# A transformer block on one Trainium2 core: a new order of tasks, q and k in three chunks, one transpose for two token streams, and load tasks tied to compute tasks

## The chip, the core and the metric

The kernel runs on one core of a Trainium2 chip. The core has five engines that run their own instruction queues and wait for each other by semaphores: PE (TensorE: a weight load, then a matmul), DVE (VectorE), ACT (ScalarE), POOL (GpSimd) and SP (SyncE, which here only issues DMAs). The metric is the device time of one execution in microseconds (us). Before the change it is 292.95 us, the median of three runs (291.63 to 293.17).

## The reference, cut to what matters

```python
S, D, H, Dh, W, dil, Fh = 2048, 448, 16, 28, 8, 2, 896
# A: sliding local attention, 8 keys at a distance of 2
q, k, v = layernorm(x) @ wqkv                    # 3 x 448 columns
logits = einsum('bhsd,bhswd->bhsw', q, k[pos - 2 * w]) * Dh ** -0.5   # masked where pos - 2w < 0
o = einsum('bhsw,bhswd->bhsd', softmax(logits), v[pos - 2 * w])
h = x + o @ wo
# B: gMLP; the tokens are mixed by a full 2048 x 2048 matrix
z = gelu(layernorm(h) @ w_in)                    # 2 x 896 columns
g = einsum('ts,bsf->btf', w_sp, layernorm(z[..., Fh:])) + b_sp[None, :, None]
out = h + (z[..., :Fh] * g) @ w_out
```

## The kernel before, in words

The 2048 tokens are two streams of 1024 (s = 0, 1), and most steps handle a **unit** u of 128 tokens of both streams at once (8 units). The steps, in the names of the program's tasks:

- `bn1`, `rs1`, `nrm1`, `tT1`, `ev1` for a unit: layernorm statistics on DVE (L612, L613), the reciprocal root on POOL (L602, L603), the normalisation into the ring `tring` on DVE (L626), transposes on PE (L636: fourteen of 64 columns, seven for each stream), and the copy into `xh` (L597 on ACT or L599 on DVE). `xh` holds stream 0 in partitions 0 to 63 and stream 1 in 64 to 127, so that a matmul over 64 rows for either stream can stand beside that of the other. 16 tokens ahead of stream 1 take the same way by themselves (`xhalo`, `thalo`, L657 to L674).
- `rpk`, `rpq`: q and k weights are copied from the staged `wqkv` into padded columns (L597, L599, and POOL's L599). `mmk`, `mmq` (L728): q and k for four groups g of heads, in chunks of 128, 256, 256, 256 and 128 tokens (`CB`), evicted by L597 or L599.
- For each of nine attention tiles i of 114 tokens: `mmv` (L768) and its eviction, `mml` (L802, 64 small matmuls: the logits), `exp` (L815, ACT), `mask` (L823, DVE), `mmr` (L832: the row sums), `mmo` (L846, 64 small matmuls), `ln` and `rex` (L856, L862, ACT: one over the sum), `ot` (L870, DVE).
- For each unit: `mmy` (L908: the product with `wo`), `h` (L916: the residual), layernorm again (`bn2`, `rs2`, `nrm2`, `tT2`, `ev2`, by the same lines), `mmz2` (L928), gelu `ge` (L938), and the layernorm of z2 (`bn3` L944, `ag3` L950, `rs3`, `nrm3` L958).
- `mmz1` (L972) and gelu `gz1` (L982); then `g` (L1009: 448 matmuls of 512 columns), `ua`, `um` (L1019, L1027), the product with `w_out` (L1038), the last addition (L1046) and the stores (L1050).

PSUM has eight banks; most steps take two at a time, so four such pairs are in play. A pair is free again when its eviction has run.

**What sets the order.** A planner (`Planner.run`) plays the tasks through with assumed durations and picks by priority; each task's instructions are then written into the queue of its engine in the order picked. A task's `deps` count in the planner alone. The semaphore waits that the chip sees are made apart from that, by `Sched.issue`, from the resources (`Res`) that an instruction reads and writes. Some resources are coarse: `reg3_old` stands for all of region `reg3` (wo, E, L and V of the attention). The loads of `b_sp` (`bb`, L990) and of `w_out` (L988) and `gz1` of f = 4 to 6 (L982) all write it, so they come one after the other. `r_wo` does the same for the four loads of `wo` (L877): each waits for the one before, and the first for a memset of the whole tile on POOL (`c_wo0`, L584).

SP issues, in this order: x, the q/k/v weights, `wo` (four DMAs), `w_in` (four, L534), sixteen transposing loads of the first half of `w_sp` (L889), `bb`, `w_out`, sixteen of the second half, the stores. ACT issues three loads at the start.

Of the kernel before, what the change touches and what calls it, by code (L numbers as in the profile page):

```python
# [1 line left out]

# [4 lines left out]
D = 448  # L7
DH = 28
FH = 896
# [3 lines left out]
NU = 8  # L13
ST = 1024
HALO = 14
# [16 lines left out]
WPEN = 40.0  # L32
# [95 lines left out]
class LazyRes:  # L128
# [6 lines left out]
    def __iter__(self):  # L135
        return iter([self.lst[self.hold[0]]])
# [28 lines left out]
class Planner:  # L165
# [4 lines left out]
    def __init__(self, pools, epochs, table_task):  # L170
        self.tasks = []
        self.pools = {k: [(0.0, s) for s in v] for k, v in pools.items()}
        self.epochs = epochs
        self.table_task = table_task

    def add(self, *a, **k):
        t = Task(*a, **k)
        self.tasks.append(t)
        return t

    def pick(self, p, n):
# [4 lines left out]
        whole = sorted((b for b in range(0, 8, 2) if b in free and b + 1 in free), key=lambda b: max(free[b], free[b + 1]))  # L186
# [19 lines left out]
    def run(self, bw=200.0, setup=1.9, t0=0.7):  # L206
# [29 lines left out]
        while ndone < len(tasks):  # L236
# [22 lines left out]
            while progress:  # L259
                progress = False  # L260
                for e in self.ENGS:
# [5 lines left out]
                    def key(t):  # L267
                        if e != "pe":
                            return t.prio
                        return t.prio + (1.5 if t.mode != pe_mode else 0.0) + WPEN * (self.pe_time(t, cr) - t.dur)  # L270
# [69 lines left out]
def bass_sequential_preLN__sliding_local_dilated__mixer_gmlp__prompt_kernel(  # L340
# [18 lines left out]
    with contextlib.ExitStack() as top:  # L359
# [3 lines left out]
        NTR = 6  # L363
        NE = 2
        NV = 3
        NL = 2
# [4 lines left out]
        tring = sb("tring", [128, NTR, D], BF16)  # L371
# [15 lines left out]
        thalo = sb("thalo", [16, D], BF16)  # L387
# [48 lines left out]
        r_tr = [Res("tr%d" % i) for i in range(NTR)]  # L436
        r_xh = [Res("xh%d" % u) for u in range(NU)]
        r_xpad0 = Res("xpad0")
        r_xpad1 = Res("xpad1")
# [4 lines left out]
        r_q = [[Res("q%d_%d" % (c, g)) for g in range(4)] for c in range(5)]  # L444
        r_k = [[Res("k%d_%d" % (c, g)) for g in range(4)] for c in range(5)]
# [38 lines left out]
        pl = Planner({"ps": range(8), "tr": range(NTR), "E": range(NE), "V": range(NV), "L": range(NL),  # L484
# [3 lines left out]
        TU = 11.0  # L488
# [74 lines left out]
        c_xpad = cst("c_xpad", [(lambda e: e.memset(xh[0:64, :, 0:HALO], 0.0), [], [r_xpad0]),  # L563
                                (lambda e: e.memset(xh[:, :, HALO + ST:XW], 0.0), [], [r_xend])], 0.4, prio=-97)
# [19 lines left out]
        c_wo0 = cst("c_wo0", [(lambda e: e.memset(wo_p[:, :, :], 0.0), [], [r_wo])], 1.65, prio=14)  # L584
# [21 lines left out]
        def ln_unit(u, which, src_deps, prio, ev_deps):  # L606
# [13 lines left out]
            tn, hold = [], []  # L620
            for n, b in enumerate(bl):
                h = []
                hold.append(h)

                def em_n(b=b, h=h):
                    iss("dve", lambda e: e.tensor_scalar(tring[:, h[0], :], x_tm[:, b, :], mv[:, b, 0:1], rs[:, b:b + 1],  # L626
                                                         ALU.subtract, ALU.mult),
                        reads=[r_x[b], rl[b]], writes=[r_tr[h[0]]])
                tn.append(add("nrm%d_%d" % (which, b), "dve", 0.31, em_n, deps=[tr], prio=prio + 0.5, acq=[("tr", 1, h)]))
            bk = []  # L630

            def em_t():
                o = bk[0] * 1024
                for c in range(NC7):
                    for s in range(2):
                        iss("pe", lambda e, c=c, s=s: e.transpose(psb[64 * s:64 * s + 64, o + 128 * c:o + 128 * c + 128],  # L636
                                                                 tring[:, hold[s][0], 64 * c:64 * c + 64], ident[:, :]),
                            reads=[r_tr[hold[s][0]], r_ident], writes=[r_bank[bk[0]]])
            tt = add("tT%d_%d" % (which, u), "pe", 0.40, em_t, deps=tn + [c_ident], prio=prio + 1.0, acq=[("ps", 1, bk)],
                     rel=[("tr", hold[0]), ("tr", hold[1])], mode="C", nmm=14)  # L640
# [10 lines left out]
        for u in range(NU):  # L651
            t_xh.append(ln_unit(u, 1, [t_x[u], t_x[u + 8]], 2.0 + 6.0 * u, ()))
            if u == 0:
                hb = []

                def em():
                    iss("dve", lambda e: e.bn_stats(sth[:, :], xhalo[:, :]), reads=[r_xhalo], writes=[r_lnh])  # L657
                    iss("dve", lambda e: e.bn_aggr(mvh[:, :], sth[:, :]), reads=[r_lnh], writes=[r_lnh])
                th = add("bnh", "dve", 0.76, em, deps=[t_xhalo], prio=9.0)
                th = add("rsh", "pool", 1.05, lambda: rstd(rsh[:, :], mvh[:, 1:2], nhalf[0:16, 0:1], [r_lnh]), deps=[th], prio=9.0)  # L660
                th = cst("nrmh", [(lambda e: e.tensor_scalar(thalo[:, :], xhalo[:, :], mvh[:, 0:1], rsh[:, 0:1], ALU.subtract, ALU.mult),
                                   [r_xhalo, r_lnh], [r_thalo])], 0.35, eng="dve", deps=[th], prio=9.5)

                def em_t():
                    o = hb[0] * 1024
                    for c in range(NC7):
                        iss("pe", lambda e, c=c: e.transpose(psb[64:128, o + 16 * c:o + 16 * c + 16],
                                                            thalo[:, 64 * c:64 * c + 64], ident[0:16, 0:16]),
                            reads=[r_thalo, r_ident], writes=[r_bank[hb[0]]])
                th = add("tTh", "pe", 0.4, em_t, deps=[th, c_ident], prio=10.0, acq=[("ps", 1, hb)], mode="C", nmm=7)  # L670

                def em_e():
                    o = hb[0] * 1024
                    iss("dve", lambda e: e.tensor_copy(xh[64:128, :, 0:HALO],  # L674
                                                       psb[64:128, o:o + 112].rearrange("p (c t) -> p c t", c=NC7)[:, :, 2:16]),
                        reads=[r_bank[hb[0]]], writes=[r_xpad1])
                t_xpad1 = add("evh", "dve", 0.17, em_e, deps=[th], prio=10.2, rel=[("ps", hb)])
# [23 lines left out]
        CB = [0, 128, 384, 640, 896]  # L701
        t_q = [[None] * 4 for _ in range(5)]
# [392 lines left out]
```

## Time and profile before

| | before |
|---|---|
| time, median of 3 runs | 292.95 us |
| the profiled execution | 293.18 us, span 291.4 us |
| PE busy | 263.4 us (90%) |
| DVE, ACT, POOL busy | 149.1, 91.4, 32.9 us |
| mean granted clock of PE | 0.940 |
| chain that ended last, by engine | PE 83%, DMA 6%, DVE 5%, issue 3%, ACT 2% |

The span runs from the first to the last instruction. A line such as `L728` is a line of the kernel before. In the chain of work, each piece has its start, its length and what it is; "issue" is time in which an engine waited for nothing that the profile shows. In the timeline, a bracket behind a row gives the idle time ahead of it and what ended it. In the windows, each row gives a stretch, its length, and the busy time of each engine with its number of instructions, then the granted clock of PE, the share of the DMA engines and GB/s.

### The profile page before, as it was taken

Reading aid. Unit: us, or ns where it says so; the run is one execution under the profiler, and the core shown is the slowest. Engines: PE = TensorE matmul, PEld = TensorE weight load, DVE = VectorE, ACT = ScalarE, POOL = GpSimd, SP = SyncE. Lnnn points to the kernel's source line nnn. Section 1 sums busy time; section 2 is a strip of 40 time slices with the busy share of each in tenths; the row PEclk is TensorE's granted clock in tenths of the full one; section 3 lists DMA queues with packets and bytes.
Section 4 is the critical chain, followed back from the end, with each engine's and each line's share of the span. In section 5 each row is a group of like instructions: output and inputs, shape, how many; then the busy total and the mean of one; then the engine's idle time right before and its main releaser. Section 6 shows DMA issues by size and latency. Waiting matters only on the chain.

```text
span 291.4 us, 7309 instructions
## 1 busy us (share of the span) xinstructions
PE 263.4 (90%) x3323; PEld 145.0 (50%) x3335; DVE 149.1 (51%) x284; ACT 91.4 (31%) x98; POOL 32.9 (11%) x78
## 2 busy tenths in 40 slices
PE   7289767998997999999938999999999999999996
PEld 2087645656765684545413444444444444444442
DVE  2886641577686865899524504333333333333333
ACT  0436833558447279763404660000000000000000
POOL 7631400012011020123110100000000000000000
PEclk9759975999999995999986999999999999999999
DMA  6946999993000000000073343333100010001001
GB/s 215 258 142 142 207 201 149 161 139 66 6 2 4 2 4 2 0 3 2 12 205 75 72 96 86 72 74 72 63 0 2 0 63 2 0 0 63 2 0 64
DMA packets 43735, 19.90 MB, mean 68 GB/s; under 512 B 34536, under 2 KB 43576, under 8 KB 43704
## 3 DMA queue, kind: packets, MB, share of 16 engines
q1 hardware_dynamic: 42632, 18.11, 30.3%
q10 hardware_dynamic: 1072, 1.32, 1.6%
q8 instruction: 26, 0.43, 0.6%
q14 instruction: 5, 0.04, 0.1%
HBM read 9.20 MB, written 1.84 MB: 38 GB/s over the span
## 4 chain that ended last, share of the span: by engine, by line
PE 83%; DMA 6%; DVE 5%; issue 3%; ACT 2%; SPq 0%; ACTq 0%
PE psum L1009 33%; PE psum L728 10%; PE psum L928 8%; PE psum L1038 7%; PE psum L972 7%; PE psum L908 4%; PE psum L768 4%; PE psum L846 3%; DMA xhalo<-in_A_x_dram 3%; PE psum L636 2%; PE psum L802 2%; DMA reg<-in_B_w_out_dram 2%; DVE reg L599 2%; DMA reg<-in_B_b_sp_dram 1%; PE psum L832 1%
## 5 line engine op out<-in xcount | busy, mean ns | idle before, releaser
L1019 DVE TENSOR_TENSOR ub<-psum,reg 128x512 bf16<-128x512 f32 x28 | 19.4, 692 | 71.5 <-PE psum L1009 71.5
L1009 PE MATMUL psum<-reg,z2p 128*128 128x512 bf16 x218 | 48.5, 379 | 0.3
L1009 PE MATMUL psum<-wspT_lo,z2p 128*128 128x512 bf16 x218 | 48.2, 379 | 0.5 <-issue 0.3
L1009 PEld LDWEIGHTS psum<-reg,z2p 128*128 128x128 bf16 x224 | 21.9, 98 | 26.4
L1009 PEld LDWEIGHTS psum<-wspT_lo,z2p 128*128 128x128 bf16 x224 | 21.6, 98 | 26.6 <-issue 0.8
L728 PE MATMUL psum<-xh,reg 64*128 64x256 bf16 (+2 forms) x560 | 31.8, 273 | 0.6 <-DVE xh L674 0.3
L928 PE MATMUL psum<-w_in,xh 64*128 64x448 bf16 x224 | 25.1, 384 | 5.3 <-ACT reg L982 5.3
L728 PEld LDWEIGHTS psum<-xh,reg 64*128 64x128 bf16 x560 | 25.0, 105 | 5.0 <-issue 0.8
L597 ACT ACTIVATE reg<-psum 128x1024 bf16<-128x1024 f32 (+2 forms) x19 | 17.0, 895 | 27.3 <-PE psum L728 17.0
L944 DVE BATCH_NORM_STATS2 st<-z2p 128x6 f32<-128x448 bf16 x32 | 17.9, 611 | 8.9 <-ACT z2p L938 8.9
L972 PE MATMUL psum<-xh,w_in 64*128 64x512 bf16 x196 | 21.9, 376 | 0.0
L1038 PE MATMUL psum<-reg 128*128 128x448 bf16 x112 | 21.8, 352 | 0.0
L602 POOL TENSOR_SCALAR rs<-mv 128x2 f32<-128x2 f32 x24 | 7.1, 297 | 126.7 <-DVE mv L613 87.9
L612 DVE BATCH_NORM_STATS2 st<-x_tm 128x6 f32<-128x448 bf16 x32 | 19.4, 605 | 2.0 <-DMA x_tm<-in_A_x_dram 1.9
L928 PEld LDWEIGHTS psum<-w_in,xh 64*128 64x128 bf16 x224 | 11.3, 102 | 18.1 <-ACT reg L982 6.0
L982 ACT ACTIVATE reg<-psum 128x1024 bf16<-128x1024 f32 x14 | 14.3, 1024 | 17.9 <-PE psum L972 10.9
L815 ACT ACTIVATE reg<-psum 128x928 bf16<-128x928 f32 x18 | 17.0, 943 | 7.8 <-PE psum L768 3.8
L603 POOL TENSOR_TENSOR rs<-rs,nhalf 128x2 f32<-128x2 f32 x24 | 17.1, 713 | 2.0
L938 ACT ACTIVATE z2p<-psum 128x896 bf16<-128x896 f32 x16 | 14.7, 917 | 7.1 <-PE psum L928 7.1
L1038 PEld LDWEIGHTS psum<-reg 128*128 128x128 bf16 x112 | 11.0, 98 | 10.4
L636 PE MATMUL psum<-ident,tring 128*64 128x128 bf16 x224 | 10.5, 239 | 6.0 <-issue 3.1
L626 DVE TENSOR_SCALAR tring<-x_tm,mv,rs 128x448 bf16<-128x448 bf16 x32 | 12.6, 432 | 6.1 <-POOL rs L603 6.0
(62 smaller groups left out, 242.9 us busy)
## 6 DMA issues: line engine op xcount, KB each, us to landing
w_in<-in_B_w_in_dram SPq DMA_DIRECT2D x4, 784.0 KB, 12.3
out_dram<-tring SPq DMA_DIRECT2D x16, 112.0 KB, 1.7
x_tm<-in_A_x_dram SPq DMA_DIRECT2D x15, 112.0 KB, 8.0
z2p<-in_A_wqkv_dram ACTq DMA_DIRECT2D x1, 784.0 KB, 7.9
z2p<-in_A_wqkv_dram SPq DMA_DIRECT2D x1, 784.0 KB, 9.4
reg<-in_B_w_out_dram SPq DMA_DIRECT2D x1, 784.0 KB, 4.8
reg<-in_B_b_sp_dram SPq DMA_DIRECT2D x1, 512.0 KB, 3.7
reg<-in_A_wqkv_dram ACTq DMA_DIRECT2D x1, 392.0 KB, 10.2
```

What stands on the lines that cost most here:

```text
L597: iss("act", lambda e: e.activation(dst, src, AF.Copy), reads=rd, writes=wr)
L603: iss("pool", lambda e: e.tensor_tensor(dst, dst, nh, ALU.pow), reads=rr + [r_nhalf], writes=rr)
L612: iss("dve", lambda e: e.bn_stats(st[:, b, :], x_tm[:, b, :]), reads=[r_x[b]], writes=[rl[b]])
L636: iss("pe", lambda e, c=c, s=s: e.transpose(psb[64 * s:64 * s + 64, o + 128 * c:o + 128 * c + 128], tring[:, hold[s][0], 64 * c:64 * c + 6 ...
L728: iss("pe", lambda e, c=c, s=s, gi=gi, lhs=lhs: e.matmul(psum[:, bk[s] * 512 + cw * gi:bk[s] * 512 + cw * gi + cw], lhs, xh[64 * s:64 * s ...
L815: iss("act", lambda e: e.activation(E[:, es[0], 2 * n:2 * n + 2, :], pair_view(lb, 2 * n, 8 * JW), AF.Exp, scale=SCALE), reads=[r_bank[lb[ ...
L928: iss("pe", lambda e, c=c, s=s: e.matmul(psum[:, zb[s] * 512:zb[s] * 512 + D], xh[64 * s:64 * s + 64, c, HALO + 128 * u:HALO + 128 * u + 128],
L944: iss("dve", lambda e, b=b: e.bn_stats(st3[:, b, k, :], z2p[:, b, D * k:D * k + D]), reads=[r_z2[b][k]], writes=[r_st3[b][k]])
L972: iss("pe", lambda e, c=c, s=s: e.matmul(psum[:, bk[s] * 512:bk[s] * 512 + 512], w_in[64 * s:64 * s + 64, c, 128 * f:128 * f + 128], xh[64 ...
L1009: iss("pe", lambda e, b=b: e.matmul(psum[:, gb[0] * 512:gb[0] * 512 + 512], z2p[:, b, 128 * f:128 * f + 128], src[:, b, 512 * (tc % 2):512 ...
L1019: iss("dve", lambda e: e.tensor_tensor(ub[:, us_[0], :], psum[:, gb[0] * 512:gb[0] * 512 + 512], bb[:, 512 * tc:512 * tc + 512], ALU.add), ...
L1038: iss("pe", lambda e, f=f: e.matmul(psum[:, wb[0] * 512:wb[0] * 512 + D], z1p[f][:, 128 * m:128 * m + 128], w_out[:, f, :], start=(f == 0) ...
```

## The change

- The priorities of nearly all tasks are moved by a table of offsets (`OFF`) and by a seeded random number; the tiles' due times lie closer (`TU` 11.0 to 7.616). The planner's costs of a change of mode and of issue-bound work on PE are higher (`MPEN`, `WPEN`).
- q and k are made in three chunks (128, 384 or 398, 512 tokens) instead of five.
- A unit's two streams are normalised into one row of `tring`, 64 columns of one beside 64 of the other, and seven transposes of 128 columns take the place of fourteen of 64.
- The four banks of the logits are taken and freed as two pairs.
- `mmo` is planned behind `ln`; the memset `c_wo0` behind the second unit's `ev1`.
- Each load of `w_in`, `w_sp`, `bb` and `w_out` gets one compute task as a dependency in the planner.

```diff
-WPEN = 40.0
+WPEN = 189.727
+MPEN = 4.564
+OFF = {"q": -19.2, "v": -12.23, "evv": -0.37, "l": -69.19, "exp": 78.83, "mask": -16.37, "r": -86.03,
+       "o": -57.86, "ln": -12.7, "ot": 3.28, "y": 6.26, "h": 35.75, "ln2": -14.24, "z2": 28.29, "ge": -10.62,
+       "n3": 22.43, "x0": 11.12, "xd": 1.15, "evq": 37.45}
+SEED, SIGMA = 806416, 0.5
+O_AFTER_LN = True
+TU = 7.616
...
     def add(self, *a, **k):
         t = Task(*a, **k)
+        if SIGMA and t.eng != "sp":
+            t.prio += self.rng.gauss(0.0, SIGMA)
...
-        NTR = 6
+        NTR = 4
-        tring = sb("tring", [128, NTR, D], BF16)
+        tring = sb("tring", [128, NTR, 2 * D], BF16)
...
-        c_wo0 = cst("c_wo0", [(lambda e: e.memset(wo_p[:, :, :], 0.0), [], [r_wo])], 1.65, prio=14)
+        c_wo0 = cst("c_wo0", [(lambda e: e.memset(wo_p[:, :, :], 0.0), [], [r_wo])], 1.65, prio=50, deps=[t_xh[1]])
...
-                    for s in range(2):
-                        iss("pe", lambda e, c=c, s=s: e.transpose(psb[64 * s:64 * s + 64, o + 128 * c:o + 128 * c + 128],
-                                                                 tring[:, hold[s][0], 64 * c:64 * c + 64], ident[:, :]),
-                            reads=[r_tr[hold[s][0]], r_ident], writes=[r_bank[bk[0]]])
+                    iss("pe", lambda e, c=c: e.transpose(psb[:, o + 128 * c:o + 128 * c + 128],
+                                                        tring[:, h[0], 128 * c:128 * c + 128], ident[:, :]),
+                        reads=r_tr[h[0]] + [r_ident], writes=[r_bank[bk[0]]])
...
-                th = add("bnh", "dve", 0.76, em, deps=[t_xhalo], prio=9.0)
+                th = add("bnh", "dve", 0.76, em, deps=[t_xhalo], prio=2.15)
...
-        CB = [0, 128, 384, 640, 896]
+        CQ = [0, 128, 512, ST]
+        CK = [0, 128, 526, ST + HALO]
...
-                                   prio=T + 0.01 * len(tls), acq=[] if tls else [("ps", 4, lb), ("E", 1, es)], mode="L", nmm=16, gate=EP_TILE[i]))
+                                   prio=T + OFF["l"] + 0.01 * len(tls), acq=([] if half else [("ps", 2, lbs[n])]) + ([] if tls else [("E", 1, es)]), mode="L", nmm=16, gate=EP_TILE[i]))
...
+        by = {t.name: t for t in pl.tasks}
+        pace = [by[n % i] for i in range(NT) for n in (("exp%d_0", "ot%d") if i else ("ot%d",))]
+        pace += [by["ge%d_%d" % (u, k)] for u in range(3) for k in range(2)]
+        later = [t_win[1, 0], t_win[1, 1], t_win[0, 0], t_win[0, 1]] + [t_wsp[b][0] for b in S_ORDER]
+        for t, d in zip(later, pace):
+            t.deps.append(d)
+        pace = [by["ge%d_%d" % (u, k)] for u in range(4, NU) for k in range(2)]
+        pace += [by["gz1_1_%d" % f] for f in range(FC7)] + [by["ua0_%d" % f] for f in range(FC7)]
+        later = [t_bb, t_wout] + [t_wsp[b][1] for b in S_ORDER]
+        for t, d in zip(later, pace):
+            t.deps.append(d)
```

**Three places in the order of instructions.** The first is SP's queue from the last loads of x on, in the changed kernel, with the semaphores that each row waits for (`sem_q..` is a DMA, `sem_pool` and `sem_pe` an engine; reg3 holds wo, later `b_sp` and `w_out`).

```order
L528 DMA x_tm<-in_A_x_dram 128x448 x12
L887 DMA reg3<-in_A_wo_dram 28x4x448 [waits sem_pool]
L887 DMA reg3<-in_A_wo_dram 28x4x448 [waits sem_q21]
L887 DMA reg3<-in_A_wo_dram 28x4x448 [waits sem_q22]
L887 DMA reg3<-in_A_wo_dram 28x4x448 [waits sem_q23]
L544 DMA w_in<-in_B_w_in_dram 64x7x896 x4
L899 DMA_TRANSPOSE wspT_lo<-in_B_w_sp_dram 128x1024 x16
L1000 DMA reg3<-in_B_b_sp_dram 128x2048 [waits sem_pe,sem_q24]
L998 DMA reg3<-in_B_w_out_dram 128x7x448 [waits sem_q45]
```

The rows of before are these, with other line numbers and the same waits: no load has a wait on a compute task that it did not have. What moved is the event that the first `wo` row waits for, the memset on POOL. POOL's rows from the first unit's reciprocal root on (rs1 of a unit is the pair with TENSOR_TENSOR, rsh is that of the 16 tokens, COPY a repack of q or k weights, MEMSET reg3 the memset `c_wo0`), before:

```order
L602 TENSOR_SCALAR rs1<-mv1 128x2 [waits sem_pool,sem_dve]
L603 TENSOR_TENSOR rs1<-rs1,nhalf 128x2 [waits sem_pool]
L584 MEMSET reg3 128x1792 [waits sem_pool]
L599 COPY reg1<-z2p 128x7x4x28 [waits sem_pool,sem_q3,sem_q2]
L599 COPY reg1<-z2p 128x7x4x28 [waits sem_pool]
L602 TENSOR_SCALAR rsh<-mvh 16x1 [waits sem_pool,sem_dve]
```

and of the changed kernel:

```order
L611 TENSOR_SCALAR rsh<-mvh 16x1 [waits sem_dve]
L612 TENSOR_TENSOR rsh<-rsh,nhalf 16x1 [waits sem_pool]
L608 COPY reg1<-z2p 128x7x4x28 [waits sem_pool,sem_q5,sem_q2]
L608 COPY reg1<-z2p 128x7x4x28 [waits sem_pool]
L611 TENSOR_SCALAR rs1<-mv1 128x2 [waits sem_pool,sem_dve]
L612 TENSOR_TENSOR rs1<-rs1,nhalf 128x2 [waits sem_pool]
L611 TENSOR_SCALAR rs1<-mv1 128x2 [waits sem_pool,sem_dve]
L612 TENSOR_TENSOR rs1<-rs1,nhalf 128x2 [waits sem_pool]
L611 TENSOR_SCALAR rs1<-mv1 128x2 [waits sem_dve]
L612 TENSOR_TENSOR rs1<-rs1,nhalf 128x2 [waits sem_pool]
L688 MEMSET reg3 128x1792 [waits sem_pool]
```

The memset moved from behind the first unit's root to behind the fourth's, and the root of the 16 tokens ahead of the two repacks. On ACT, the second half of the q/k weights (`wqk1`) now stands behind half of the v weights (`wv1`); before it stood ahead of it.

The second place is PE in the attention, where q and k of the third chunk are made (L728, in the changed kernel L738), between row sums (L832, now L842), `mmo` (L846, now L862), logits (L802, now L813) and `mmy` (L908). Before:

```order
L846 MATMUL psum<-reg 32x58 x32
L728 MATMUL psum<-xh,reg 128x256 x28
L846 MATMUL psum<-reg 32x58 x32
L832 MATMUL psum<-reg,ones 32x464 x8
L728 MATMUL psum<-xh,reg 128x256 x28
L846 MATMUL psum<-reg 32x58 x32
L908 MATMUL psum<-reg 128x448 x8
```

and in the changed kernel:

```order
L738 MATMUL psum<-xh,reg 128x512 x14
L862 MATMUL psum<-reg 32x58 x32
L738 MATMUL psum<-xh,reg 128x512 x14
L862 MATMUL psum<-reg 32x58 x32
L738 MATMUL psum<-xh,reg 128x512 x14
L842 MATMUL psum<-reg,ones 32x464 x8
L813 MATMUL psum<-reg 64x58 x32
L738 MATMUL psum<-xh,reg 128x512 x14
L813 MATMUL psum<-reg 64x58 x32
L738 MATMUL psum<-xh,reg 128x512 x14
```

Groups of 14 long matmuls took the place of 28 shorter ones, and a row sum or 16 to 32 small matmuls stand between two of them.

The third place is PE from the last two `mmy` (L908, now L918) to the end of z1 (`mmz2` is L928, now L938; `mmz1` L972, now L982; `g` L1009, now L1019; `tT2` L636, now L643). Before:

```order
L972 MATMUL psum<-xh,w_in 128x512 x56
L1009 MATMUL psum<-wspT_lo,z2p 128x512 x12
L908 MATMUL psum<-reg 128x448 x8
L636 MATMUL psum<-ident,tring 64x128 x14
L1009 MATMUL psum<-wspT_lo,z2p 128x512 x4
L972 MATMUL psum<-xh,w_in 128x512 x14
L928 MATMUL psum<-w_in,xh 128x448 x28
L636 MATMUL psum<-ident,tring 64x128 x14
L972 MATMUL psum<-xh,w_in 128x512 x14
L928 MATMUL psum<-w_in,xh 128x448 x28
L972 MATMUL psum<-xh,w_in 128x512 x112
```

and in the changed kernel:

```order
L918 MATMUL psum<-reg 128x448 x8
L938 MATMUL psum<-w_in,xh 128x448 x56
L918 MATMUL psum<-reg 128x448 x8
L938 MATMUL psum<-w_in,xh 128x448 x28
L982 MATMUL psum<-xh,w_in 128x512 x98
L643 MATMUL psum<-ident,tring 128x128 x7
L1019 MATMUL psum<-wspT_lo,z2p 128x512 x2
L643 MATMUL psum<-ident,tring 128x128 x7
L1019 MATMUL psum<-wspT_lo,z2p 128x512 x2
L938 MATMUL psum<-w_in,xh 128x448 x56
L982 MATMUL psum<-xh,w_in 128x512 x98
```

The last `mmy` moved ahead of all of z1 and of the last two tasks of z2's sixth unit; all seven z1 tasks of the first half now follow in one piece, and the z2 of the last two units stands between the halves.

More of the change, by code (lines that the diff above doesn't have):

```diff
@@ L1 @@
 import contextlib
+import random
 import concourse.bass as bass
@@ L135, in __iter__ @@
     def __iter__(self):
-        return iter([self.lst[self.hold[0]]])
+        return iter(self.lst[self.hold[0]])
 class Task:
@@ L185, in pick @@
             return sorted(sorted(free, key=lambda s: (free[s], s))[:n]) if len(free) >= n else None
-        whole = sorted((b for b in range(0, 8, 2) if b in free and b + 1 in free), key=lambda b: max(free[b], free[b + 1]))
+        whole = sorted((b for b in range(0, 32, 2) if b in free and b + 1 in free), key=lambda b: max(free[b], free[b + 1]))
         if n == 1:
@@ L750, in bass_sequential_preLN__sliding_local_dilated__mixer_gmlp__prompt_kernel, with chunks @@
                         (t_q if isq else t_k)[ch][g0 + gi] = te
-        def chunks(lo, hi):
-            return [c for c in range(5) if CB[c] < hi and (c == 4 or CB[c + 1] > lo)]
+        def chunks(cb, lo, hi):
+            return [c for c in range(3) if cb[c] < hi and (c == 2 or cb[c + 1] > lo)]
         t_v = []
```

162 lines of the change are left out of this document (81 added, 81 removed).

## The prediction

> **What bounds the kernel now.** I read the page's busy times first, then the chain of work in order of time, and then the timeline around every gap in the chain.
>
> ```profile
> PE 263.4 (90%) x3323; PEld 145.0 (50%) x3335; DVE 149.1 (51%) x284; ACT 91.4 (31%) x98; POOL 32.9 (11%) x78
> 174.14 10.74 PE psum L1009 x49
> ```
>
> PE is the bound: 263.4 of 291.4 us. From 174.14 on it runs the long matmuls of L1009 and L1038 without a gap, and the change leaves those as they are. What can change lies before 174 us: 28.0 us of idle PE, and stretches in which PE is busy but slow. Four places hold most of it. The first is the start:
>
> ```profile
> 2.02 8.87 DMA xhalo<-in_A_x_dram
> 14.75 0.28 DVE thalo L661
> 15.92 3.17 PE psum L728 x56
> ```
>
> The 16 tokens land at 10.89, but DVE normalises them only at 14.75, behind repacks and other statistics, and the first q/k matmul starts at 15.92. The second and third place are two stalls of the same kind:
>
> ```profile
> 37.63 0.36 PE L636 MATMUL psum<-ident,tring 128*64 128x128 bf16 x6 [3.07 <-issue]
> 42.48 0.22 PE L802 MATMUL psum<-reg 32*64 32x58 bf16 x2
> 45.74 0.66 PE L802 MATMUL psum<-reg 32*64 32x58 bf16 x30 [3.04 <-issue]
> 38.00:40.00 2.00, 2.00 (x52) 1.27 (x56) 1.92 (x4) 0.00 (x0) 0.00 (x0) 0.54 1.07 199
> q8 instruction: 26, 0.43, 0.6%
> q8 instruction: 1, 0.02, 8.8%
> ```
>
> PE stops in the middle of a group of transposes and in the middle of a group of logits, waiting for nothing. It looks like missing code: the page's 26 transfers of instructions come to 6658 (3323 matmuls, 3335 weight loads) over 26, or 256, and between the two stalls lie just 128 pairs. The last row is the one such transfer that starts between 34 and 35 us; the DMA engines were full then with the loads of `w_in` (share 1.07 in the row of 38 to 40 us). A piece seems to be asked for when the piece before it is begun: one begun at 28.9 us (counted by pairs) came at 37.63, one begun at 37.63 came at 45.74, so 8.1 to 8.7 us under `w_in`. Both times PE then ran at a clock of 0.5 for some 4 us. Together this place costs 6.1 us idle and about 4.4 us of half clock. The fourth place is behind the attention:
>
> ```profile
> 142.64 1.53 PE psum L908 x8
> 144.25 3.67 DMA reg<-in_B_b_sp_dram
> 147.94 4.79 DMA reg<-in_B_w_out_dram
> 152.81 1.03 ACT reg L982
> 153.89 2.80 PE L928 MATMUL psum<-w_in,xh 64*128 64x448 bf16 x14 [5.31 <-ACT reg L982]
> 156.69 0.89 PE psum L636 x14
> ```
>
> The last `mmy` ends at 144.17. Only then do `bb` and `w_out` load, one after the other, 8.6 us until ACT may run the gelu that shares their resource. PE runs out of banks and idles 5.3 us, then runs at half clock.
>
> **The change part by part**, against the profiled execution's 293.18 us.
>
> *The gap at `w_out`: -7.2.* In the new order 2 tasks of z2 and 5 of z1 stand between the last `mmy` and the matmuls of the gelu that waits.
>
> ```profile
> 112.85 17.90 PE psum L928 x168
> 133.79 6.16 PE psum L972 x56
> 129.49 0.92 ACT L938 ACTIVATE z2p<-psum 128x896 bf16<-128x896 f32 x1 [0.41 <-PE psum L928]
> ```
>
> ACT's gelu rows in this stretch are 1.325 us apart, the pace of one z2 task at full clock; a z1 task is 6.16 / 4 = 1.54. So PE has 2.65 + 7.7 = 10.4 us of work against 8.6 us of loads. The gap closes with 1.8 us to spare: -5.3. With it goes the half clock behind it: 2.80 instead of 1.33, and 0.89 instead of 0.51, -1.9. If the loads came 2 us late, 0.2 us of it would come back. What hides the loads is PE's work alone.
>
> *q and k: -1.7.* The chunk of 128 stays.
>
> ```profile
> 54.44 1.64 PE psum L728 x28
> 101.65 1.68 PE psum L728 x56
> 94.83 1.54 PE L728 MATMUL psum<-xh,reg 64*128 64x142 bf16 x42
> 87.90 0.60 PE L728 MATMUL psum<-xh,reg 64*128 64x142 bf16 x14 [0.29 <-ACT reg L597]
> ```
>
> At full clock a task of 28 with 256 columns takes 1.64, so the other chunks now cost 12 x 1.64 + 1.68 + 1.54 + 0.60 = 23.5. After it, 14 of 512 columns take 1.54 as z1's do, 384 and 398 in proportion 1.16 and 1.20: 8 x 1.54 + 4 x 1.16 + 4 x 1.20 = 21.8.
>
> *Transposes: -1.0.* Fourteen take 0.51:
>
> ```profile
> 104.95 0.51 PE psum L636 x14
> L636 PEld LDWEIGHTS psum<-ident,tring 128*64 128x64 bf16 x224 | 7.8, 120 | 9.3 <-issue 4.3 <-DVE tring L626 2.4 <-DVE reg L599 1.1
> L1009 PEld LDWEIGHTS psum<-reg,z2p 128*128 128x128 bf16 x224 | 21.9, 98 | 26.4
> L636 PE MATMUL psum<-ident,tring 128*64 128x128 bf16 x224 | 10.5, 239 | 6.0 <-issue 3.1 <-DVE tring L626 1.2 <-DVE reg L599 1.0
> ```
>
> The 128-column matmuls of q and k above need 1.68 / 28 = 0.06 per pair side by side; seven full-width transposes at that pace need 0.42, 0.09 less, at most 1.4 for 16 units. The other end is no overlap (a rival below). I take -1.0, near the q/k row, since a weight load of 128 columns shows no more time (98 ns) than one of 64 (120 ns). The Trainium skill (TensorE: Matmul & The Clock Gate, "LDWEIGHTS") lets a weight load grow with its columns, 128 / 1.2 ns, so that seven double loads would cost what fourteen cost now, and this term would be 0; the two rows do not show that growth.
>
> *The start: -1.2.* DVE now takes the 16 tokens first, and POOL their root ahead of the repacks.
>
> ```profile
> 13.09 0.57 POOL L603 TENSOR_TENSOR rsh<-rsh,nhalf 16x1 f32<-16x1 f32 x1
> 9.16 1.28 ACT L597 ACT_TABLE_LOAD   x1 [9.16 <-DMA z2p<-in_A_wqkv_dram]
> 10.68 2.35 ACT L597 ACTIVATE reg<-z2p 128x784 bf16<-128x784 bf16 x3 [0.23 <-DMA z2p<-in_A_wqkv_dram]
> reg<-in_A_wqkv_dram ACTq DMA_DIRECT2D x1, 392.0 KB, 10.2
> ```
>
> The root, now done at 13.66 behind POOL's repacks, can be done 0.8 earlier, at 12.9, and the normalisation follows at once instead of at 14.75: the tokens are ready at 15.92 - 1.85, about 14.1. But ACT's queue now moves `wv1` ahead of `wqk1`. The last of ACT's three loads is issued at 1.96 and lands at 1.96 + 10.2 = 12.2; that place is `wqk1`'s in the new order, so ACT's table load (1.28, at 9.16 now) begins there, and its first repack (2.35 / 3) is done at 14.3. The first q/k matmul needs both, and a repack of DVE's behind the normalisation; I put it at 14.7 instead of 15.92. Ends: -1.9 if `wqk1` shares bandwidth more kindly, +0.5 if it lands at 14.
>
> *The loads: 0.* The paced dependencies make no semaphore wait: SP's rows are the same. The only true delay is `c_wo0`, now behind the fourth root.
>
> ```profile
> 19.67 0.27 POOL L602 TENSOR_SCALAR rs<-mv 128x2 f32<-128x2 f32 x1 [0.44 <-DVE mv L613]
> 7.49 1.59 POOL L584 MEMSET reg<- 128x1792 bf16 x1
> 18.00 5.42 SPq L877 DMA_DIRECT2D reg<-in_A_wo_dram  x3
> 23.46 3.65 SPq L534 DMA_DIRECT2D w_in<-in_B_w_in_dram  x4
> ```
>
> The fourth root begins at 19.67 now and about 21 after; with 1.0 for it, 1.6 for the memset and four serial `wo` loads of 2.45 each (three took 5.42 with the last only issued), `w_in` is issued at about 31 instead of 23.46 and holds the DMA engines from 33 to 50. By the order, PE begins pieces of code near 39 us (end of the second q/k chunk) and some 4 to 8 us later, amid transposes, logits and small matmuls, where a piece lasts only 4 to 5 us. Both ask under `w_in`, so I expect one long and one short stall in place of two of 3 us: no gain. Ends: -10.5 if PE meets no such stall, +4 if both are 5 us.
>
> *The attention: -1.0.* Small matmuls in a long run cost more than behind a long matmul:
>
> ```profile
> 98.78 1.42 PE psum L846 x64
> 58.57 0.27 PE psum L846 x32
> ```
>
> 64 in one run take 1.42, 32 behind a long group 0.27. The new order has few runs above 32: four or five split runs save about 3. Against it, in the 17 us of the third q/k chunk DVE gets six of eight evictions of 1024 elements (1.23 each), three masks (1.13) and three `ot` (1.23): 14.5 us of work in an in-order queue, so PE will wait there for banks, about 2. Ends: -4, if more of the runs are split at no wait, and +6, if a third of that DVE work stands in the way of PE.
>
> *z2 of the last units: +1.0.* On DVE `h6` and `h7` now stand behind the statistics of six units.
>
> ```profile
> 124.59 2.15 DVE L944 BATCH_NORM_STATS2 st<-z2p 128x6 f32<-128x448 bf16 x4
> 126.66 0.92 DVE L958 TENSOR_SCALAR z2p<-z2p,mv,rs 128x896 bf16<-128x896 bf16 x2
> ```
>
> A unit costs DVE 3.1, PE 2.65. Counted from z2's start, DVE reaches `h6` at about 25, and `nrm2` of unit 6 at about 32; PE ends the first seven z1 tasks at about 32. They meet, with 0 to 4 of wait; I take 1.0. The half clock at z2's start (17.90 for 12 tasks against 15.9) I leave as it is. Only 0.86 us of idle stood ahead of it; the Trainium skill (TensorE: Matmul & The Clock Gate, "Why this matters for your kernels") asks for gaps above about 3 us before the clock falls. By that rule nothing of it would be left to expect, and the sum would be 2.0 lower.
>
> **Sum:** -7.2 - 1.7 - 1.0 - 1.2 + 0 - 1.0 + 1.0 = -11.1, so 282.1 on the profiled execution. That execution lies 0.2 above the median of 292.95, so I forecast **281.9**.
>
> **The rivals.** *The stalls for code go* (0.20): chunks of 512 columns use less code in a microsecond, and `w_in` comes later. Then 10.5 less: 271.4. For it: no stall in the trace falls outside `w_in`. Against: about 17 us of `w_in` hold two pieces. *The attention waits more* (0.16): DVE near its bound in the third chunk, pairs of banks short; the end at +6 gives 281.9 + 7 = 288.9. Against: between the logits and the row sums of a tile stands 2 to 5 us of other PE work, against 0.94 + 1.13 of `exp` and mask. *Transposes do not overlap* (0.07): today's overlap may come from the two halves of 64 columns. Seven at 239 ns take 1.67, not 0.51: 16 x 1.16 = 18.6, with the -1.0 gone: 301.5, **slower**. It decides from 0.51 + 12 / 16 = 1.26 for seven, 180 ns each. The skill's page on TensorE gives 275 ns for a full transpose in a kernel (Part 4), which without overlap would be worse still. Against: L1009 and L908 load full-width weights beside running matmuls.
>
> **How the numbers follow.** Forecast 0.55, the rivals 0.20, 0.16, 0.07, other 0.02. The range reaches from 270.5 (stalls gone) to 290.5 (attention at its upper end), and leaves out the transposes and the outer parts of the others, under 0.2. A measurement can tell 0.5% from no change: faster takes the forecast, the first rival and most of the second, 0.87; same 0.05; slower 0.08.
>
> **What would show it.** ACT's L992 waiting for no `w_out`, and no PE gap behind the last `mmy`; L738 at 1.5 per 14 of 512 columns; L643 at about 0.45 for seven; the first L738 at 14 to 15 us; `w_in` issued at 29 to 33 and PE gaps marked "issue" between 38 and 55; the first `tT2` after z1 within 2 us. I am wrong if pieces of code come late at other places, or if the new order leaves PE waiting on DVE for more than 6 us in the attention.

## The result, and the profile after

| | before | after |
|---|---|---|
| time, median of 4 runs | 292.33 us | 276.62 us (273.63 to 277.22) |
| ratio | | 0.944, 95% interval 0.936 to 0.952 |
| the profiled execution | 293.18 us, span 291.4 | 273.63 us, span 271.7 |
| from the first q/k matmul to z2's start | 96.9 us | 87.3 us |
| from z2's start to the end of z1 | 61.3 us | 49.0 us |
| mean granted clock of PE | 0.940 | 0.962 |

The kernel is 15.7 us faster by the medians. The two traced executions lie further apart, 19.6 us: the two stretches of the table gave 21.9, the part behind them grew by 2.6, since 12 gating matmuls moved into it, and the start is 0.5 shorter. A ratio, here and below, compares only executions within 1.5% of the fastest one of their kernel, which leaves out two of four in one experiment, the early load of `w_in`. First the busy row of the page, then rows of PE's timeline, of the changed kernel:

```profile
PE 253.5 (93%) x2987; PEld 129.5 (48%) x2999; DVE 149.5 (55%) x283; ACT 90.7 (33%) x100; POOL 33.2 (12%) x78
```

```profile
15.41 5.67 PE L738 MATMUL psum<-xh,reg 64*128 64x128 bf16 x112 [0.94 <-DVE xh L683]
45.02 0.30 PE L813 MATMUL psum<-reg 32*64 32x58 bf16 x5 [1.60 <-issue]
53.68 0.22 PE L862 MATMUL psum<-reg 64*32 64x58 bf16 x7 [1.55 <-issue]
118.93 1.69 PE L918 MATMUL psum<-reg 128*128 128x448 bf16 x8
120.55 2.82 PE L938 MATMUL psum<-w_in,xh 64*128 64x448 bf16 x28
123.21 10.75 PE L982 MATMUL psum<-xh,w_in 64*128 64x512 bf16 x98
133.89 0.56 PE L643 MATMUL psum<-ident,tring 128*128 128x128 bf16 x7
```

Behind the last `mmy` (118.93) no bracket is left: PE goes on with z2 and z1 while `bb` and `w_out` load, as the issues of the two loads and ACT's gelu of the fifth z1 task show:

```profile
120.72 0.37 SPq L1000 DMA_DIRECT2D reg<-in_B_b_sp_dram  x1
124.37 0.40 SPq L998 DMA_DIRECT2D reg<-in_B_w_out_dram  x1
131.00 1.02 ACT L992 ACTIVATE reg<-psum 128x1024 bf16<-128x1024 f32 x1 [0.49 <-PE psum L982]
```

`w_out` lands 4.8 us after its issue, at 129.2, and this gelu, the first that shares its resource, starts 1.8 us later and waits for PE alone. The first transposes behind z1 (133.89) wait for nothing either. Two gaps "issue" ahead of z2 are left, 3.15 us in place of 6.11, and behind the first the half clock again. The windows (length, PE's busy time and instructions, granted clock, DMA share, GB/s):

```profile
44.00:46.00 2.00, 0.98 (x13) 0.58 1.05 196
46.00:48.00 2.00, 2.00 (x24) 0.50 1.08 214
48.00:50.00 2.00, 2.00 (x64) 0.50 1.41 189
50.00:52.00 2.00, 2.00 (x37) 0.71 1.76 160
```

And the groups of PE's lines with the total of each:

```profile
L738 PE MATMUL psum<-xh,reg 64*128 64x128 bf16 (+3 forms) x336 | 29.8, 338 | 1.1 <-DVE xh L683 0.9
L938 PE MATMUL psum<-w_in,xh 64*128 64x448 bf16 x224 | 22.3, 349 | 0.0
L862 PE MATMUL psum<-reg 64*32 64x58 bf16 x576 | 8.7, 192 | 2.1 <-issue 1.5 <-ACT reg L826 0.5
```

The same groups took 31.8 (q and k), 25.1 (z2) and 11.7 us (`mmo`) before.

### The profile page after: what moved, and what is told of

Same layout as the page of the kernel before. It is cut to its first block, busy times and chain, and to the rows that moved or that the text cites. A ratio compares the mean times of both kernels' runs of the same rounds, so it can differ in the third digit from the quotient of the medians.

```text
span 271.7 us, 6639 instructions
## 1 busy us (share of the span) xinstructions
PE 253.5 (93%) x2987; PEld 129.5 (48%) x2999; DVE 149.5 (55%) x283; ACT 90.7 (33%) x100; POOL 33.2 (12%) x78
## 4 chain that ended last, share of the span: by engine, by line
PE 85%; DVE 5%; DMA 4%; issue 2%; ACT 2%; POOL 1%; SPq 0%
PE psum L1019 35%; PE psum L738 11%; PE psum L938 8%; PE psum L1048 8%; PE psum L982 8%; PE psum L918 4%; DMA xhalo<-in_A_x_dram 4%; PE psum L813 3%; PE psum L778 3%; PE psum L643 2%; PE psum L862 2%; DVE st L621 1%; ACT reg L826 1%; DVE tring L632 1%; PE psum L842 1%
## 5 line engine op out<-in xcount | busy, mean ns | idle before, releaser
L1019 PE MATMUL psum<-reg,z2p 128*128 128x512 bf16 x218 | 48.7, 379 | 0.3
L1019 PE MATMUL psum<-wspT_lo,z2p 128*128 128x512 bf16 x218 | 48.4, 379 | 0.4 <-issue 0.2
L1019 PEld LDWEIGHTS psum<-reg,z2p 128*128 128x128 bf16 x224 | 21.9, 98 | 26.2
L1019 PEld LDWEIGHTS psum<-wspT_lo,z2p 128*128 128x128 bf16 x224 | 21.7, 98 | 26.1 <-issue 0.4
L738 PE MATMUL psum<-xh,reg 64*128 64x128 bf16 (+3 forms) x336 | 29.8, 338 | 1.1 <-DVE xh L683 0.9
L1048 PE MATMUL psum<-reg 128*128 128x448 bf16 x112 | 22.3, 352 | 0.0
L938 PE MATMUL psum<-w_in,xh 64*128 64x448 bf16 x224 | 22.3, 349 | 0.0
L606 ACT ACTIVATE reg<-psum 128x896 bf16<-128x896 f32 (+4 forms) x20 | 16.8, 842 | 14.7 <-PE psum L738 8.6
L982 PE MATMUL psum<-xh,w_in 64*128 64x512 bf16 x196 | 21.5, 375 | 0.0
L738 PEld LDWEIGHTS psum<-xh,reg 64*128 64x128 bf16 x336 | 15.8, 110 | 10.6 <-issue 1.1
L611 POOL TENSOR_SCALAR rs<-mv 128x2 f32<-128x2 f32 x24 | 6.1, 252 | 103.4 <-DVE mv L622 78.2
L948 ACT ACTIVATE z2p<-psum 128x896 bf16<-128x896 f32 x16 | 14.7, 917 | 9.6 <-PE psum L938 9.2
L632 DVE TENSOR_SCALAR tring<-x_tm,mv,rs 128x448 bf16<-128x448 bf16 x32 | 15.0, 490 | 3.4 <-POOL rs L612 3.2
L938 PEld LDWEIGHTS psum<-w_in,xh 64*128 64x128 bf16 x224 | 10.9, 94 | 10.1 <-issue 0.8
L778 PE MATMUL psum<-reg,xh 64*64 64x448 bf16 x252 | 14.9, 378 | 0.5 <-DVE xh L608 0.5
```

The source lines that it names most:

```text
L632: iss("dve", lambda e: e.tensor_scalar(tring[:, h[0], :].rearrange("p (c s f) -> p s c f", c=NC7, s=2)[:, n], x_tm[:, b, :].rearrange("p ( ...
L738: iss("pe", lambda e, c=c, s=s, gi=gi, lhs=lhs: e.matmul(psum[:, bk[s] * 512 + cw * gi:bk[s] * 512 + cw * gi + cw], lhs, xh[64 * s:64 * s ...
L778: iss("pe", lambda e, c=c, s=s, w=w: e.matmul(psum[64 * w:64 * w + 64, bk[s] * 512:bk[s] * 512 + D], xh[64 * s:64 * s + 64, c, a + w:a + w ...
L938: iss("pe", lambda e, c=c, s=s: e.matmul(psum[:, zb[s] * 512:zb[s] * 512 + D], xh[64 * s:64 * s + 64, c, HALO + 128 * u:HALO + 128 * u + 128],
L982: iss("pe", lambda e, c=c, s=s: e.matmul(psum[:, bk[s] * 512:bk[s] * 512 + 512], w_in[64 * s:64 * s + 64, c, 128 * f:128 * f + 128], xh[64 ...
L1019: iss("pe", lambda e, b=b: e.matmul(psum[:, gb[0] * 512:gb[0] * 512 + 512], z2p[:, b, 128 * f:128 * f + 128], src[:, b, 512 * (tc % 2):512 ...
```

## The experiments

Twelve kernels ran. In those with a recorded order, the planner's order is kept and only the named tasks move or wait, so that nothing else in the program is rearranged; their line numbers are higher by a constant of each kernel (L838 in the one with quarters is L813). The runs came in three batches on three chips, each beside the kernel before: the first four (291.72 us), the fourteen transposes to the quarters (292.37), and the last four (291.72). Medians of different batches are therefore best read with their ratios.

**The gap at `w_out` alone, in the kernel before.**

```diff
-    gelu of z1, f >= 4:  writes=[r_z1[f][ch], r_z1[f][2 + ch]] + old
+    gelu of z1, f >= 4:  writes=[r_z1[f][ch], r_z1[f][2 + ch]], after=old
-    bb, w_out:           writes=[...] + reg3_old
+    bb, w_out:           writes=[..., r_ser], after=reg3_old
```

`after` waits for a resource's users without becoming its writer.

> The kernel before, with one dependency less: the gelu tasks of f >= 4 no longer count as writers of the resource that bb and w_out write, while bb and w_out keep their order. My theory (the gap at w_out is a dependency, worth 5.3 us of idle PE and 1.9 us of half clock): ACT's gelu no longer waits, the PE gap of 5.31 us is gone, and the kernel takes 285 to 287 against about 293 (ratio 0.975 to 0.985). Rival: another wait takes its place (banks, or the loads themselves collide) and less than 3 us is won, 290 or more.

285.45 us against 291.72, ratio 0.977 (0.974 to 0.981): 6.3 us won, 5.5 to 7.7 by the interval. The timeline of PE around the place that held 5.31 us of idle time:

```profile
143.94 1.69 PE L973 MATMUL psum<-xh,w_in 64*128 64x512 bf16 x14
145.47 2.81 PE L929 MATMUL psum<-w_in,xh 64*128 64x448 bf16 x28
148.21 0.58 PE L637 MATMUL psum<-ident,tring 128*64 128x128 bf16 x14
```

No gap and no half clock. The dependency was the cause, and no other wait took its place.

**Real waits for the later loads, in the changed kernel.** In the change, pacing is known to the planner alone. Here the load waits on the chip for its task.

```diff
+PACED = {'win1_0': ['ot0'], 'win1_1': ['exp1_0'], 'win0_0': ['ot1'], 'win0_1': ['exp2_0'], ...}
```

> The changed kernel in its own order, but each later load (w_in, w_sp, bb, w_out) really waits on the chip for the compute task by which the planner paces it, so w_in is issued at about 58 instead of 31.5. My theory (PE's stalls at 43.4 and 52.1 are code that is late under w_in): both stalls, 3.15 us together, and some of the half clock of 44 to 51 go, and w_in's bursts at 58 to 75 bring back at most one stall of 1.5; 2 to 5 us less than the changed kernel. Rival A: pieces of code come late whatever the loads do: the same time within 1 us. Rival B: the stalls only move to 58 to 75, where PE's pieces are short: 0 to 2 us more.

270.32 us, ratio 0.927 (0.923 to 0.931); the changed kernel on the same chip (the run after the next) took 275.09. So 4.8 us were won, as my theory had it, but not by the way I wrote: the first `ot` ends at 34, not at 58, and `w_in` is spread rather than late:

```profile
34.42 18.13 SPq L565 DMA_DIRECT2D w_in<-in_B_w_in_dram  x4
```

Two stalls of 1.02 and 0.97 us were left.

**The load of `w_in` early again, in the changed kernel.**

```diff
     rs1_0
+    c_wo0
     ...
-    c_wo0    (behind rs1_3)
```

> The changed kernel in its own order, but the memset of wo's pads stands on POOL behind the first root again, so that wo is issued at about 18 and w_in at about 23.5, as before the change. My theory: PE's pieces of code are asked for under w_in either way, one or two stalls of 1.5 to 3 us each, the total within 1.5 us of the changed kernel. Rival: the delay of w_in is what cut the stalls from 6.1 to 3.15 us, and 3 to 5 us come back.

The four executions took 270.18, 271.81, 274.63 and 275.47 us. Their median, 273.22, lies 1.9 below the changed kernel beside it, and the traced one (274.63) has stalls of 1.12 and 3.04 us; the ratio of 0.928 (0.922 to 0.933) rests on the first two alone. My bound of 1.5 was missed, on the fast side. The rival falls: the one delay that the change really makes on a load, from 23.5 to 31.5, saves nothing, and if anything costs.

**The changed kernel again.**

> The changed kernel unchanged, beside the others on one chip: about 276.6, and its ratio to the kernel before 0.937 to 0.952.

275.09 us, ratio 0.941 (0.936 to 0.946). Its trace beside the first one's tells more than its time. PE's timeline:

```profile
14.57 5.01 PE L738 MATMUL psum<-xh,reg 64*128 64x128 bf16 x112 [1.64 <-DVE xh L683]
43.01 0.24 PE L813 MATMUL psum<-reg 32*64 32x58 bf16 x5 [1.08 <-issue]
52.49 0.25 PE L862 MATMUL psum<-reg 64*32 64x58 bf16 x7 [4.79 <-issue]
97.97 0.57 PE L862 MATMUL psum<-reg 64*32 64x58 bf16 x32 [0.52 <-ACT reg L826]
98.90 1.67 PE L918 MATMUL psum<-reg 128*128 128x448 bf16 x8 [0.36 <-ACT reg L850]
```

The same program stops at the same two matmuls, but for 5.87 us together instead of 3.15, and has the full clock at 98.90, where the first trace shows 2.85 us for the same eight matmuls at half clock. From the first q/k matmul to z2's start both took 87.3 us. Sizes of single stalls are those of an execution; their places are those of the program.

**Fourteen transposes in place of seven, and q and k in half chunks, each in the changed kernel.**

```diff
-    e.transpose(psb[:, ...128], tring[:, h[0], 128 * c:128 * c + 128], ident)
+    for s in range(2):
+        e.transpose(psb[64 * s:64 * s + 64, ...128], tring[:, h[0], 128 * c + 64 * s:...+ 64], ident)
```

> The changed kernel in its own order, but each unit is transposed by fourteen matmuls of 64 columns instead of seven of 128, as before the change. My theory (a matmul pair costs its issue, not its width): a unit takes 0.5 to 0.64 us instead of 0.42 to 0.55, 1.0 to 1.9 us more in all, and up to 1.5 more or less because 112 more pairs move the borders of the pieces of code. Rival: seven wide weight loads cost what fourteen narrow ones do: no change of the transposes, within 0.5 us but for the code.

```diff
+    for x0, x1 in ((0, cw // 2), (cw // 2, cw)) if ch else ((0, cw),):
         for c in range(NC7):
             for s in range(2):
-                e.matmul(psum[... cw], lhs, xh[..., t0:t0 + cw])
+                e.matmul(psum[... x0:x1], lhs, xh[..., t0 + x0:t0 + x1])
```

> The changed kernel in its own order, but the q and k tasks of the second and third chunk run each weight twice, over half of the columns (256 or 192 and 199), which brings back 224 pairs of code. My theory (the chunks are worth little by themselves, 0.2 to 1.7 us of matmul time): 0.2 to 2 us more, with another stall or two of 1.5 us possible from the code. Rival: wider chunks are a main source of the gain, through less code in each microsecond: 4 us or more lost, with stalls as long as before the change.

277.35 us (ratio 0.950, 0.944 to 0.956) and 279.29 us (0.956, 0.951 to 0.961), against 0.941 for the changed kernel. Neither settles a price, since both traces hold longer stalls for code than the first trace of the changed kernel (2.01 and 4.03 us; 3.77 and 3.28 us). They had to be run again without stalls.

**Real waits in the kernel before.**

```diff
+PACED = {'win1_0': ['ot0'], 'win1_1': ['exp1_0'], 'win0_0': ['ot1'], 'win0_1': ['exp2_0'], 'wsp0_0': ['ot2'], ...}
```

> The kernel before in its own order, but each quarter of w_in and each block of the first half of w_sp really waits on the chip for a compute task of the attention (w_in from the first ot on). My theory (both stalls of 3 us are code that is late under w_in, and the half clock behind them follows from the stalls): the stalls at 34.6 and 42.7 go, 6.1 us, and up to 4.4 us of half clock with them: 283 to 288 against 293. Rival: the stalls move under the later loads: within 2 us of the kernel before.

289.03 us, ratio 0.988 (0.984 to 0.993): less gain than I expected, and near the rival. The stalls are at 49.30 and 61.51 instead, 3.26 us together in place of 6.11, and z2 begins at 106.69 instead of 112.79. So 6.1 us were won there, and then partly lost again, as the chain shows:

```profile
139.10 0.01 PE psum L996
139.11 4.84 DMA reg<-in_B_b_sp_dram
143.97 4.73 DMA reg<-in_B_w_out_dram
```

My own waits on `w_sp` kept SP busy until 139.1, and `bb` stood behind them, with the last `w_sp` block under way: the gap at `w_out` became 7.82 us instead of 5.31. The run tests two things at once, and the second was my fault.

**One quarter of `w_in` at a time, in the changed kernel.**

```diff
+PACED = {'win1_0': ['ot0'], 'win1_1': ['ot1'], 'win0_0': ['ot2'], 'win0_1': ['ot3'], 'wsp0_0': ['exp4_0'], ...}
```

> The changed kernel in its own order, with each quarter of w_in waiting on the chip for an ot of its own (the first four), and the blocks of the first half of w_sp for later tasks of the attention, so that no burst is longer than some 4 us. My theory: no piece of code waits behind more than one quarter, no stall over 1 us is left, 3 to 6 us less than the changed kernel. Rival: any load in the attention delays code there, and as much stall comes back: within 1 us.

268.03 us (267.37 to 269.0), ratio 0.917 (0.913 to 0.921), 7.1 us below the changed kernel of the first batch, beyond what I expected. No gap "issue" of 0.2 us or more is left before z2. PE from 28 to 60 us (windows), first of the changed kernel's second trace, then of this one:

```profile
28.00:60.00 32.00, 25.99 (x544) 0.95 0.92 159
```

```profile
28.00:60.00 32.00, 30.82 (x695) 1.00 0.28 61
```

The same span holds 4.8 us more of work, at full clock. This is the fastest kernel of the study, 8% below the kernel before.

**Two moves at the start, on top of that.**

```diff
 ACT queue:  x8, 
-            wv1, wqk1
+            wqk1, wv1
 DVE:        nrmh,
-            rp (two), evh, rp (two)
+            evh, rp (four)
```

> The changed kernel with w_in paced by quarters as before, and two moves at the start: on ACT's queue the second half of the q/k weights is loaded ahead of that of v, as before the change, and DVE copies the 16 normalised tokens (evh) ahead of its first repack. My theory (the first q/k matmul waits for the load of the q/k weights, or for evh behind two repacks, whichever is later): it starts at 13.5 to 14.5 instead of 15.2, and 0.5 to 1.5 us are won, 266.5 to 267.5. Rival: the 16 tokens land late (10 to 11.7 us), DVE then stands idle in front of evh and its repacks come later: no gain.

269.18 us, ratio 0.922 (0.919 to 0.926): no gain. PE's first q/k matmul came at 15.64 instead of 15.19, and its bracket names a repack of DVE:

```profile
15.64 2.63 PE L775 MATMUL psum<-xh,reg 64*128 64x128 bf16 x46 [1.56 <-DVE reg L645]
```

The moved half of the weights was there at 10.5 (13.65 before the move), but DVE stood in front of the 16 tokens, which landed at 11.36, and repacked only at 14.28. The rival holds.

**Both faults out of the kernel before**, the first as in the first experiment, `w_in` by quarters (`ot0` to `ot3`) and `w_sp` behind the last.

> The kernel before in its own order, with both faults taken out: the gelu freed of bb and w_out, and each quarter of w_in waiting on the chip for an ot of its own (w_sp behind the last). My theory: the two savings add, 6.3 from the gap (as measured alone) and 6 from the stalls (z2 began 6.1 earlier with w_in paced): 278 to 282, so that of the changed kernel's gain some 6 to 7 us is the gap and about 3 the stalls. Rival: the savings overlap, or the half clocks stay: 284 or more.

276.56 us (275.19 to 278.29), ratio 0.948 (0.943 to 0.953). More than the sum that I expected: 8.9 us below the kernel without the gap. No stall is left, and no gap of PE behind the first q/k matmul is above 0.97 us, in the old order, with the old chunks and transposes. By time this is the changed kernel over again (276.62). Its `mmo` and `mml` groups, and those of the fastest kernel, both without stalls:

```profile
L870 PE MATMUL psum<-reg 64*32 64x58 bf16 x576 | 12.0, 190 | 1.2 <-DVE reg L623 0.7 <-issue 0.3 <-ACT reg L880 0.2
L826 PE MATMUL psum<-reg 32*64 32x58 bf16 x576 | 12.1, 191 | 0.5 <-ACT xh L621 0.4
```

```profile
L838 PE MATMUL psum<-reg 32*64 32x58 bf16 x576 | 11.4, 191 | 0.6 <-ACT reg L631 0.5
L887 PE MATMUL psum<-reg 64*32 64x58 bf16 x576 | 8.6, 193 | 0.5 <-ACT reg L851 0.5
L763 PE MATMUL psum<-xh,reg 64*128 64x128 bf16 (+3 forms) x336 | 28.9, 331 | 2.4 <-DVE xh L708 2.3
```

As many small matmuls, of the same mean length, cover 24.1 us in the old order and 20.0 in the new one; the next two runs show that this is not the order's doing alone.

**The prices of transposes and chunks without stalls**, the two edits above on top of the quarters.

> The changed kernel with w_in paced by quarters, so without stalls for code, and fourteen transposes of 64 columns a unit instead of seven of 128. My theory: their own price alone, 16 times 0.1, 1.0 to 1.9 us more than with seven. Rival: the price is in the code (112 pairs more), so that a stall comes back: 3 us or more.

> The changed kernel with w_in paced by quarters, and the q and k tasks of the second and third chunk in two halves of their columns. My theory: the price of short chunks alone, 0.2 to 2 us more, with no stall over 1 us. Rival: code: 224 pairs more bring a stall back, 3 us or more.

269.68 us (ratio 0.924, 0.921 to 0.928) and 269.28 us (0.923, 0.920 to 0.926), against 268.03 (0.917): 1.65 and 1.25 us more by the medians, with at most 0.46 us of "issue" in any gap. But the kernel with quarters ran in another batch. From the first q/k matmul to the end of z1, its trace has 131.89 us and these two have 132.97 and 132.82: 1.1 and 0.9 more. (The kernel of the start moves, in their own batch, has 132.07.) So the theories hold, the first at its lower edge. The price doesn't stand in the lines that were edited. A group of fourteen transposes takes 0.58 us where seven take 0.56, and q and k keep their sum of 28.9, as the row of the kernel with half chunks shows beside the row above. What grew are the small matmuls. First `mml` with fourteen transposes, then q and k, `mml` and `mmo` with half chunks:

```profile
L839 PE MATMUL psum<-reg 32*64 32x58 bf16 x576 | 12.5, 191 | 0.7 <-ACT reg L631 0.5
```

```profile
L764 PE MATMUL psum<-xh,reg 64*128 64x256 bf16 (+3 forms) x560 | 28.9, 262 | 2.1 <-DVE xh L708 1.9
L839 PE MATMUL psum<-reg 32*64 32x58 bf16 x576 | 11.9, 192 | 1.1 <-ACT reg L631 0.5 <-issue 0.5
L888 PE MATMUL psum<-reg 64*32 64x58 bf16 x576 | 9.7, 190 | 0.5 <-ACT reg L852 0.5
```

With fourteen transposes `mml` and `mmo` together cover 21.4 us (12.5 and 8.9), with half chunks 21.6, instead of 20.0. In the timelines the growth is in the runs that stand right behind the edited work: 32 of `mmo` behind transposes take 1.13 instead of 1.00, twice, and 32 behind a half chunk of 256 columns up to 0.55 instead of 0.34. The records share out time between pipelined neighbours, so the sum of the edited group alone would have priced either edit at next to nothing.

## Why the prediction held, and which of its terms were off

The kernel got faster as forecast, and 276.6 lies in the range; the forecast of 281.9 was 5.3 too high, about the size of the last row. Term by term, by the medians:

| term | forecast | the runs | by |
|---|---|---|---|
| gap at `w_out` | -7.2 | -6.3 | the dependency removed alone |
| q and k in wide chunks | -1.7 | -1.25 (-0.9 in the traces) | half chunks, without stalls |
| transposes | -1.0 | -1.65 (-1.1 in the traces) | fourteen again, without stalls |
| start | -1.2 | -0.5 | first q/k matmul, mean of traces |
| stalls for code | 0 | -0.3 to -1.8 | stalls removed from both kernels |
| attention and z2 | -1.0 + 1.0 | about -5 (-3.3 in the traces) | what is left |

*The gap.* Right, with its reason. Where the forecast gave 1.9 us of half clock on top of 5.3, the whole came to 6.3, with 5.5 to 7.7 open.

*Chunks and transposes.* Near in size, but by another way than I wrote. I expected the time in their own rows: 14 of 512 columns at 1.54 us, seven transposes at 0.42. They take 1.62 and 0.50 in the chain, hardly less in sum than the old ones; the saving shows in the small matmuls behind them.

*Stalls for code.* The step said that both kernels would meet stalls, at new places and of about the same total, and they do: taking them out saves 8.9 us before the change (285.45 to 276.56) and 7.1 to 8.6 after it (275.09 or 276.62 to 268.03). The mechanism holds too: they go when `w_in` comes one quarter at a time. The rival by which they vanish did not come about, since the change paces `w_in` in the planner's model only. Stalls cost more than their gaps, 8.9 us for 6.4 of idle time (3.05 and 3.31 in the kernel without the gap), as the half clock behind them had suggested.

*Start.* The first q/k matmul came at 15.41 and 14.57 in the two traces of the changed kernel, around the 14.7 of the forecast; over nine traces of kernels with the changed start its mean is 15.0, over four with the old one 15.6. The chain to it goes through the 16 tokens in the first trace, which landed at 11.73 where I had 10.89, and through `wqk1` in the second, which landed at 13.03 where I had 12.2.

*Attention: -1.0, the step that failed.* Its second half, 2 us of PE waiting for DVE in the third chunk of q and k, did not come. DVE was as full as I counted, in the changed kernel (busy times of PE, PEld, DVE, ACT and POOL):

```profile
59.80:77.00 17.20, 16.96 (x434) 8.81 (x435) 13.65 (x17) 9.54 (x12) 0.93 (x2) 1.00 0.95 155
```

13.65 of 17.2 us, and yet PE was busy for 16.96. A busy share of 0.8 in order is no wait; I had taken fullness for lateness without following one bank. Over the whole stretch from the first q/k matmul to z2's start, PE idled 5.7 us in the old order without its two faults and 3.6 in the new order without stalls: 2.1 less, where the step had 2 more. Its first half, 3 us from split runs of small matmuls, isn't shown. The small matmuls do cover 4.1 us less (24.1 to 20.0), but the transposes move 1.4 of that and the chunks 1.6; if the two add, 1.1 is left for the split runs.

*z2: +1.0, the other step.* No wait came at 133.89. The half clock that I left at z2's start has not gone, it has moved. The rows of z2 are shorter (25.1 to 22.3 us, of which 1.7 is the gap's: 23.4 in the old order without it), but the eight matmuls of `mmy` at 98.60, a little ahead of z2, take 2.85 us. They take 2.85 to 3.15 in nine of the ten traces of kernels in the new order; the second trace of the changed kernel, with 1.67, is the exception. The Trainium skill (TensorE: Matmul & The Clock Gate, "Why this matters for your kernels") asks for gaps above about 3 us before the clock falls, which would have put the sum 2.0 lower and nearer to the result. But the rule isn't what these traces show: gaps of 0.48 to 0.53 and 0.34 to 0.36 us stood ahead of these eight matmuls in all ten.

What stays open: the size of the last row. By the medians about 5 us are left. In the two traces without stalls, the old order takes 139.84 us from the first q/k matmul to the end of z1 and the new one 131.89; of the 8.0 between them 2.6 are gating matmuls and 2.0 the two edits, so 3.3 are left, most of it the 2.1 of idle time. No run joins the split runs again. And why one execution of ten has the full clock at 98 us wasn't found.

## What to carry to other kernels

A gap that ends with a wait on an engine which itself waits for a load is worth a look at the resource that ties them: one edit took 6.3 us out, and with the paced loads it is worth, in the old order, as much as the whole change. Pacing that only a planner knows doesn't hold a queue back; a semaphore on each quarter of a load does. And price an edit in a version without stalls, since code that shifts by a hundred instructions moves a stall of several microseconds.

## What the runs showed of the hardware

Where PE stops depends on the count of its instructions, and for how long on the execution. The nine traces with stalls, of kernels in both orders and with different loads, hold two each, and the number of matmuls ahead of each, with as many weight loads, is 478, 479, 606, 607, 734, 862, 990 or 1117: steps of 128, up to one or two, or 256 instructions, which is also what the page's 26 transfers of instructions hold each in the kernel before. That such a transfer came late isn't seen directly; the steps, and the end of the stalls when the loads are spread, speak for it. In the changed kernel the same two places cost 1.60 and 1.55 us in one execution, 1.08 and 4.79 in another. With the quarters of `w_in` apart, the DMA share from 28 to 60 us was 0.28 instead of 0.92 to 0.94, five transfers of instructions were moved there as against four and five, and PE shows no gap "issue" there.

The clock behind a stall goes by its length only in part. In these nine traces all nine gaps "issue" of 3.04 us or more have a granted clock of about 0.5 behind them for some 3 us or longer, and all six of 1.55 us or less have the full clock. In between, that of 1.60 had it halved for 6 us and that of 2.01 until the next gap, but that of 1.91 had it full. And at the end of the attention, behind many small matmuls, gaps of 0.5 and 0.35 us had half clock behind them in nine traces of ten.
